# Piece size of loads, order of weight transfers and slot size in a fused linear-attention and mixture-of-experts kernel

## The chip, the cores and the metric

The kernel runs on one core of one Trainium2 chip. The metric is the device time of one execution in microseconds. Other engines than TensorE (PE) are named as the profile names them: DVE (VectorE), ACT (ScalarE), POOL (GpSimd), SP (SyncE).

## The reference

Linear attention with decay over blocks of 64 positions, then a top-1 mixture of experts on its output. Batch 4, 8 heads, 768 positions, head size 64; that makes 3072 tokens of 512 numbers, 8 experts with a hidden size of 1024.

```python
for b in range(nb):                       # blocks of 64 positions
    intra = (qb @ kb.T * Dmask) @ vb      # Dmask[i, j] = lam ** (i - j) for i >= j
    inter = (qb * lam_pow) @ kv_state
    out[:, :, block] = intra + inter
    kv_state = lam ** 64 * kv_state + (kb * rev_pow).T @ vb
x = out.transpose(0, 2, 1, 3).reshape(3072, 512)
logits = x @ w_gate + modality_bias[modality_id]
e_idx = argmax(logits); gate_w = softmax(logits)[e_idx]
for e in range(8):                        # each token goes to one expert
    out[mask] = gate_w[mask] * (relu(x[mask] @ w1[e]) @ w2[e])
```

## The kernel before, in words

**Attention stage.** The kernel works in 24 blocks of 128 positions (6 per batch element). A loop over steps `g` from 0 to 25 is a pipeline written out by hand: step `g` prepares block `g + 1` (`prepare`: two DVE products, `qd` on L200 and `kd` on L205), computes the scores of block `g` (`scores`, PE on L220, masks on DVE L223), the outputs of block `g - 1` (`from_state` L258, `outputs` L269, copies on ACT L271), adds to the state (`carry`, L235), and turns block `g - 2` into tokens (`tokens`): PE transposes them together with the router's product (L281), ACT copies the result to a tile `xn` (L282, three buffers), ACT's queue stores that tile to a table `xs` in HBM (L283, 256 KB), and DVE sums the logits (L285).

**Loads.** K, Q, V and a second layout of K lie together in the input `qkv`. One load (L180, on SP's queue) brings two blocks: a tile of 128 partitions with 16 KB each, contiguous in HBM. There are twelve such tiles in three buffers; the first comes in four parts (L68, L90), the next two follow in step 0, and from step 2 on every second step issues the load whose buffer the outputs of the step have just freed (the last, number 11, in step 18). In the same queue stand the two decay tables `dk` (L84, read from a small table that ACT's queue has written), and the filling of the slot table with an end mark (`inv<-pad`, L162, four transfers of 384 and 392 KB).

**Routing.** After the last block of a batch element `route` picks each token's expert on DVE, and a step later `route_places` works out each token's slot in its expert's list. `write_slots` then scatters 128 slots per call (POOL, L355) into the table `inv`, whose rows of `SW` = 16 words hold token number and gate weight. For two tiles of 256 tokens that can be formed from the first two batch elements, `early_list` (in step `early` = 14) makes a small list on DVE (`listA`): expert, place in `inv`, and whether the expert differs from the one before. SP reads such a list into registers (`value_load`, L517, L520, L495).

**Early tiles.** In step 18 SP fetches the two tiles' slots (`fetch_idx`, L500) and the first tile's `w1` (L525, four pieces of 512 KB into `raw1`), in step 20 its `w2` (L531, into `raw2`). POOL gathers the tokens (`fetch_rows`, L508). ACT and DVE split weights and tokens into a high and a low part (`split`, L482 and L483), and PE makes three products of each pair (`three`, L548, L551, L552).

**Expert stage.** `run(0)` and `run_early(1)` work the early tiles, two thin tiles of up to 64 tokens stand inside `run_early`, and `run(4)` and later ones work the wide tiles of 256 tokens. `run(0)` also places the last batch element's tokens and makes the list of all other tiles (`late_list`, DVE). `fetch_w1` and `fetch_w2` move nothing where the tile has the same expert as the one before; they are issued all the same. A thin tile uses plain products (`thin_first`, L578, `thin_second`, L600), and its weights come into `w1h` and `w1l` (`fetch_both`, L641, L644). `turn_rows` (L541) transposes the tokens of the next tile.

**What sets the order.** Each engine works its own instructions in the order that the build puts down. `behind(later, first)` orders two instructions: with `wait` the later one waits for the first one's end, without it the two are only put in this order.

Of the kernel before, what the change touches and what calls it, by code (L numbers as in the profile page):

```python
# [6 lines left out]
F32 = mybir.dt.float32  # L7
# [8 lines left out]
P = 128  # L16
B, H, S, D = 4, 8, 768, 64
NP = H // 2
NC = S // P
HB = 2  # L20
LOADS = 3
# [10 lines left out]
MAX_WIDE = 17  # L32
LIST = THIN + MAX_WIDE + 2
PAD = 4096
SW = 16
EMPTY = E * CAP // TT


def linear_attention_moe(tc, qkv, lam, modality, wg, mbias, w1, w2, out):
    nc = tc.nc  # L40
    with ExitStack() as ctx:
# [10 lines left out]
        def behind(later, first, wait=True):  # L52

            info = (mybir.DependencyInfo(mybir.DependencyClass.Sync, mybir.DependencyReason.DATA) if wait else
                    mybir.DependencyInfo(mybir.DependencyClass.NoSync, mybir.DependencyReason.SCHED_ONLY))
            tc.add_manual_dep(later.ins, first.ins.name, info, reason="order")
# [4 lines left out]

        def load_tile():

            return work.tile([P, HB, 4, H * D], F32, name="load", bufs=LOADS)

        first = load_tile()
        for part in (slice(0, 2), slice(2, 4)):
            nc.sync.dma_start(out=first[:, 0, part], in_=qkv[0, 0][:, 0, part])  # L68
        busy = const.tile([P, DM], BF16, name="busy")
        nc.vector.memset(busy, 0.0)  # L70
        tab = const.tile([H, 2 * P], F32, name="tab")
# [9 lines left out]

        dk = const.tile([P, 2, NP, P], F32, name="dk")
        for hl in range(2):
            tables = nc.sync.dma_start(  # L84
                out=dk[:, hl],
                in_=bass.AP(tensor=tab_d.tensor, offset=tab_d.offset + hl * 2 * P,
                            ap=[[1, P], [4 * P, NP], [1, P]]),
            )
        for part in (slice(0, 2), slice(2, 4)):
            ld = nc.sync.dma_start(out=first[:, 1, part], in_=qkv[0, 0][:, 1, part])  # L90
            behind(ld, tables, wait=False)
            tables = ld

# [81 lines left out]
        nc.vector.memset(ohsum, 0.0)  # L175

        def load_half(g):
            b, h = divmod(g, NC // HB)
            t = load_tile()
            behind(nc.sync.dma_start(out=t, in_=qkv[b, h]), tables, wait=False)  # L180
            return t

        halves = {0: first}

        def loaded(g):

            t = halves[g // HB][:, g % HB]
            kt, qt = (t[:, i].rearrange("p (a t) -> p a t", a=NP) for i in range(2))
            return kt, qt, t[:, 2], t[:, 3]

# [82 lines left out]

        def tokens(g, xt, lg):
            c = g % NC
            xn = work.tile([P, NP, P + E], F32, name="xn", bufs=3)
            for hf in range(2):
                xp = ps.tile([P, 2, 256], F32, name="x", bufs=2)
                for j in range(2):
                    p = hf * 2 + j  # L280
                    nc.tensor.matmul(xp[:, j, : P + E], xt[:, p, :], iw[:, p, :], start=True, stop=True)  # L281
                copies.append(nc.scalar.copy(out=xn[:, 2 * hf : 2 * hf + 2, :], in_=xp[:, :, : P + E]))  # L282
            nc.scalar.dma_start(out=xs[g * P : (g + 1) * P, :].rearrange("t (p d) -> t p d", p=NP),  # L283
                                in_=xn[:, :, :P])
            logits.append(nc.vector.tensor_reduce(out=lg[:, c, :], in_=xn[:, :, P:].rearrange("p q e -> p e q"),  # L285
                                                  axis=AX, op=ALU.add))
# [204 lines left out]
        def item(lst, row, i):  # L491
            return lst[0:1, row, i : i + 1] if isinstance(i, int) else lst[0:1, row, i]

        def fetch_idx(lst, i, idx, cols=TT):
            vr = nc.sync.value_load(item(lst, 1, i), min_val=0, max_val=E * CAP)  # L495
            if cols < TT:
                for p in range(0, P, cols):
                    nc.sync.dma_start(out=idx[p : p + cols, 0, :], in_=inv[bass.ds(vr, cols), 0:2])
                return
            nc.sync.dma_start(out=idx, in_=inv[bass.ds(vr, TT), 0:2].rearrange("(t p) c -> p t c", t=2))  # L500

        def groups(cols):

# [28 lines left out]
                if after is not None:  # L532
                    behind(ld, after)

        def turn_rows(cols, before=None):
            for i in range(2):
                tp = ps.tile([P, 2, TT], F32, name="x", bufs=2)
                for j in range(2):
                    kc = 2 * i + j
                    for t, m in groups(cols):  # L540
                        mm = nc.tensor.transpose(out=tp[:, j, t * P : t * P + m],  # L541
                                                 in_=xg[t][:m, kc * P : (kc + 1) * P], identity=ident[:m, :m])
                        if before is not None:
                            behind(mm, before, wait=False)
                split(tp[:, :, :cols], xh[i][:, :, :cols], xl[i][:, :, :cols])
# [150 lines left out]
        for g in range(0, ng + 2):  # L696
            if 1 <= g < ng - 1:
                st0[g + 1] = prepare(g + 1)
            if g == 2:
                routing_constants()  # L700
            if g < ng:
                st1[g], masked = scores(g)
            if g == 0:
                spread_powers()
                keep_busy(14)
                behind(nc.sync.dma_start(out=iw[:, :, P:], in_=wg), tables, wait=False)
                for i in range(1, LOADS):
                    halves[i] = load_half(i)
                for i in range(2):
                    st0[i] = prepare(i, masked)  # L710
            if 1 <= g <= ng:
                st2[g - 1], passed = outputs(g - 1, st1.pop(g - 1), from_state(g - 1, st0[g - 1][0]))
            if g < ng:
                passed = carry(g, st0[g][1]) or passed

            if g >= HB and g % HB == 0 and LOADS - 1 + g // HB < ng // HB:
                halves[LOADS - 1 + g // HB] = load_half(LOADS - 1 + g // HB)
            if g >= 2:
                b, c = divmod(g - 2, NC)
                if c == 0:  # L720
                    lgs[b] = work.tile([P, NC, E], F32, name="lg", bufs=2)
                tokens(g - 2, st2.pop(g - 2), lgs[b])
                if routed is not None:
                    slots = route_places(*routed)
                    routed = None
                if c == NC - 1:
                    routed = (b, *route(b, lgs.pop(b)))

            few = 2 if early <= g < early + 3 else 1
            write_slots(slots[:few], passed)  # L730
            slots = slots[few:]

            if g == early:
                exA, nA = early_list()
                er, _ = fetch_regs(listA, 0, True)
            elif g == early + 4:
                for i in range(EARLY):
                    fetch_idx(listA, i, idxA[i])
                fetch_w1(er, {})
            elif g == early + 6:  # L740
                fetch_w2(er, {})
            elif g == ng - 2:
                fetch_rows(idxA[0], TT, SOON * S, after=fades[-1])
            elif g == ng:
                split(raw1[0], w1h[0], w1l[0], late=True)
                turn_rows(TT)
            elif g == ng + 1:
                for i in range(1, 4):
                    split(raw1[i], w1h[i], w1l[i], late=True)
                fetch_w1(*fetch_regs(listA, 1, False))  # L750
                fetch_rows(idxA[1], TT, SOON * S)
# [11 lines left out]
        def regs(n):  # L763
            return fetch_regs(*tiles[n][1:], False)
# [21 lines left out]
        def run(n):  # L786
            idx = idxs.get(n) or get_idx(n)
            begun, turned = wide(tail, before)
            if n == 0:
                write_slots(route_places(*routed, begun))  # L790
                late_list(exA, nA)
            if n + 1 < fixed_ones:
                ahead = range(EARLY, wides + 1) if n == 0 else range(n + 2, min(n + 3, fixed_ones))
                for m in ahead:
                    idxs[m] = get_idx(m)
                fetch_w2(*regs(n + 1))
                turn_rows(TT, turned)
                for m in ahead:
                    gathered = rows_of(m)
                for i in range(4):  # L800
                    split(raw1[i], w1h[i], w1l[i])
                if n + 2 < fixed_ones:
                    fetch_w1(*regs(n + 2), gathered)
            second(idx)

        def run_early(n):
# [10 lines left out]
            fetch_w1(*regs(wides))  # L817
            other, mm = thin_first(xf[1], both[0])
            hnt = [thin_turn(hn, mm)]
            turn_rows(TT)  # L820
            gathered = rows_of(wides + 1)
            mm = thin_second(idxs[EARLY], hnt[0], raw2)
            hnt.append(thin_turn(other, mm))
            fetch_w2(*regs(wides))
            before = thin_second(idxs[EARLY + 1], hnt[1], both[1])
            w1h, w1l = parts(F32R)
# [75 lines left out]
```

## Time and profile before

| | us |
|---|---|
| median of 3 runs | 448.57 |
| lowest, highest | 447.22, 452.23 |
| profiled execution | 450.08 |
| its span | 448.3 |
| PE busy | 416.4 (93%) |
| DVE, ACT, POOL busy | 247.6, 188.1, 105.6 |

The mean granted clock of PE in the profiled execution is 0.973. The profile's page cuts the span into 40 slices of 11.2 us; a digit is the busy share of a slice in tenths, and PEclk the clock that PE was granted. In rows of the trace the first number is the start and the second the duration in us, then engine, line and operation, `out<-in`, and in brackets how long the engine sat idle before it and what ended that. An engine name with a q is that engine's instruction queue, for example while it issues a transfer.

The attention stage goes from the start to about 134 us, the early and thin tiles to about 205 us, the wide tiles to the end.

### The profile page before, as it was taken

How to read it: one execution, taken by the hardware profiler on the slowest of the kernel's cores; microseconds unless marked ns; L12 is line 12 of the kernel's file. 1: busy time of each engine (PE TensorE's matmuls, PEld its weight loads, DVE VectorE, ACT ScalarE, POOL GpSimd, SP SyncE). 2: the span in 40 equal slices, each digit the busy share in tenths (PEclk: the TensorE clock that was granted, in tenths of full speed). 3: DMA queues.
4: the chain of work that ended last, by engine and by line, in shares of the span. 5: the costliest groups of instructions: out<-in, count | busy, mean ns of one | idle time of the engine just before them, and what ended most of it. 6: DMA issues, size and time to landing. Idle time of an engine off the chain costs nothing.

```text
span 448.3 us, 9446 instructions
## 1 busy us (share of the span) xinstructions
PE 416.4 (93%) x3635; PEld 364.9 (81%) x3636; DVE 247.6 (55%) x481; ACT 188.1 (42%) x298; POOL 105.6 (24%) x110
## 2 busy tenths in 40 slices
PE   8899699899789998989999999999999999999980
PEld 4688588788669896759898999999998989898960
DVE  4686566756547946027837282919090919182510
ACT  1223133233158514134746363637272819182510
POOL 3110134431450343103221111313122221201010
PEclk9999889999898999999999999999999999999995
DMA  4999949778932012741112667530202020100000
GB/s 144 425 362 418 321 134 322 265 258 307 370 109 72 2 52 55 251 176 53 48 48 59 223 215 257 173 109 24 73 9 86 2 94 7 58 25 25 25 29 16
DMA packets 30356, 63.90 MB, mean 143 GB/s; under 512 B 6997, under 2 KB 20701, under 8 KB 28896
## 3 DMA queue, kind: packets, MB, share of 16 engines
q1 hardware_dynamic: 12816, 44.14, 27.7%
q0 software_dynamic: 4800, 12.79, 8.5%
q10 hardware_dynamic: 12688, 6.30, 4.7%
q8 instruction: 30, 0.49, 0.5%
q14 instruction: 22, 0.18, 0.1%
HBM read 91.04 MB, written 14.64 MB: 236 GB/s over the span
## 4 chain that ended last, share of the span: by engine, by line
issue 44%; PE 17%; DMA 16%; DVE 8%; POOL 7%; SPq 3%; ACT 1%; another core or an unknown queue 1%; POOLq 0%; ACTq 0%; DVEq 0%
DMA idx<-inv 4%; PE x L281 4%; POOL out_dram L622 4%; PE s L220 4%; PE o L269 4%; DMA xs<-xn 4%; POOL xg L508 3%; DMA xg<-xs,idx 3%; DMA load<-in_qkv_dram 2%; PE o L258 2%; DVE w1l L483 2%; DMA inv<-pay,sloti 2%; PE kv L235 2%; SPq L525 1%; DMA dk<-tab_d 1%
## 5 line engine op out<-in xcount | busy, mean ns | idle before, releaser
L548 PE MATMUL s<-xh,w1h 128*128 128x256 f32 x384 | 108.6, 283 | 0.8 <-issue 0.8
L551 PE MATMUL s<-xl,w1h 128*128 128x256 f32 x384 | 108.4, 282 | 0.0
L552 PE MATMUL s<-xh,w1l 128*128 128x256 f32 x384 | 108.2, 282 | 0.0
L483 DVE TENSOR_TENSOR w1l<-raw,w1h 128x1024 fp32r<-128x1024 f32 x48 | 58.0, 1220 | 75.1 <-ACT w1h L482 73.1
L551 PE MATMUL o<-w2l,hh 128*128 128x512 f32 x192 | 74.8, 390 | 2.0 <-DVE w2l L483 2.0
L548 PE MATMUL o<-w2h,hh 128*128 128x512 f32 x192 | 75.8, 395 | 0.0
L552 PE MATMUL o<-w2h,hl 128*128 128x512 f32 x192 | 74.9, 390 | 0.0
L548 PEld LDWEIGHTS s<-xh,w1h 128*128 128x128 f32 x384 | 72.6, 189 | 1.8 <-issue 1.4
L551 PEld LDWEIGHTS s<-xl,w1h 128*128 128x128 f32 x384 | 72.8, 190 | 0.4
L552 PEld LDWEIGHTS s<-xh,w1l 128*128 128x128 f32 x384 | 72.7, 189 | 0.1
L483 DVE TENSOR_TENSOR w2l<-raw,w2h 128x1024 fp32r<-128x1024 f32 x48 | 58.4, 1219 | 2.7 <-ACT w2h L482 2.2
L482 ACT CAST w1h<-raw 128x1024 fp32r<-128x1024 f32 x48 | 49.7, 1052 | 22.2 <-PE s L551 22.2
L482 ACT CAST w2h<-raw 128x1024 fp32r<-128x1024 f32 x48 | 49.8, 1041 | 0.1
L508 POOL DMA_INDIRECT xg<-xs,idx x20 | 27.7, 1383 | 83.7 <-PE x L541 80.0
L567 DVE SCALAR_TENSOR_TENSOR hl<-s,hh 128x512 fp32r<-128x512 f32 x48 | 32.9, 686 | 24.6 <-ACT hh L566 24.6
L621 ACT ACTIVATE y<-o,idx 128x512 f32<-128x512 f32 x20 | 13.8, 689 | 76.1 <-PE o L552 42.8
L622 POOL DMA_INDIRECT out_dram<-y,idx x20 | 21.4, 1068 | 101.0 <-ACT y L621 101.0
L551 PEld LDWEIGHTS o<-w2l,hh 128*128 128x128 f32 x192 | 36.1, 188 | 9.7 <-DVE w2l L483 2.5
L552 PEld LDWEIGHTS o<-w2h,hl 128*128 128x128 f32 x192 | 36.0, 188 | 7.5
L548 PEld LDWEIGHTS o<-w2h,hh 128*128 128x128 f32 x192 | 36.0, 188 | 7.1
L271 ACT COPY xt<-o 128x256 f32<-128x256 f32 x48 | 17.8, 372 | 54.8 <-PE o L269 47.9
L566 ACT ACTIVATE hh<-s 128x512 fp32r<-128x512 f32 x48 | 28.5, 594 | 23.2 <-PE s L552 13.7
(192 smaller groups left out, 505.4 us busy)
## 6 DMA issues: line engine op xcount, KB each, us to landing
raw<-in_w_dram SPq DMA_DIRECT2D x104, 512.0 KB
load<-in_qkv_dram SPq DMA_DIRECT2D x11, 2048.0 KB
xs<-xn ACTq DMA_DIRECT2D x24, 256.0 KB
load<-in_qkv_dram SPq DMA_DIRECT2D x4, 512.0 KB
w1h<-in_w_dram SPq DMA_DIRECT2D x4, 512.0 KB
w1l<-in_w_dram SPq DMA_DIRECT2D x4, 512.0 KB
inv<-pad SPq DMA_DIRECT2D x2, 392.0 KB
inv<-pad SPq DMA_DIRECT2D x2, 384.0 KB
```

The source lines that it names most:

```text
L220: nc.tensor.matmul(sps[hl][:, p, :], kt[r, p, :], qt[r, p, :], start=True, stop=True)
L269: mm = nc.tensor.matmul(op[half][place(p, hl), i, :], vt[:, (2 * p + hl) * D : (2 * p + hl + 1) * D], pts[hl][:, p, :], start=(c == 0 and ...
L281: nc.tensor.matmul(xp[:, j, : P + E], xt[:, p, :], iw[:, p, :], start=True, stop=True)
L482: cp = nc.scalar.copy(out=hi, in_=src)
L483: df = nc.vector.tensor_tensor(out=lo, in0=src, in1=hi.bitcast(F32), op=ALU.subtract)
L508: last = nc.gpsimd.indirect_dma_start(out=(to or xg)[t][:m], out_offset=None, in_=xs[:rows, :], in_offset=bass.IndirectOffsetOnAxis(ap=idx ...
L548: mm = nc.tensor.matmul(out, ah, bh, start=first, stop=False)
L551: nc.tensor.matmul(out, ah, bl, start=False, stop=False)
L552: return nc.tensor.matmul(out, al, bh, start=False, stop=last)
L566: act = nc.scalar.activation(out=hh[i], in_=hp, func=AF.Relu)
L567: nc.vector.scalar_tensor_tensor(out=hl[i], in0=hp, scalar=0.0, in1=hh[i].bitcast(F32), op0=ALU.max, op1=ALU.subtract)
L622: sc = nc.gpsimd.indirect_dma_start(out=out, out_offset=bass.IndirectOffsetOnAxis(ap=idx[:, t, 0:1], axis=0), in_=y, in_offset=None, bound ...
```

## The change

- The input `qkv` is laid out with the four arrays apart, so that a load takes 4 KB contiguous pieces, four per partition, in place of one of 16 KB; the tile's axes follow. The first tile's four parts take 2 KB pieces. The bytes are the same.
- The first of the two `dk` tables is issued on ACT's queue, the second stays on SP's.
- `xn` has four buffers in place of three.
- Slots in `inv` have 8 words (32 bytes) in place of 16, which halves the fill with end marks.
- `early_list` and the reading of its first entry move from step 14 to step 15.
- The fetches of the early slots are ordered behind the last load, and the first early tile's `w1` and `w2` wait for the last load to land.
- In `run(0)` the second early tile's `w2` is issued ahead of the slot fetches of the next tiles in place of behind them.
- In `run_early` the transposes of the next tile are cut in two: the second half goes between the two second products of the thin tiles, and the gather of the tile after it behind that.

```diff
-SW = 16
+SW = 8
@@ load tiles
-            return work.tile([P, HB, 4, H * D], F32, name="load", bufs=LOADS)
+            return work.tile([P, 4, HB, H * D], F32, name="load", bufs=LOADS)
+
+        def source(g):
+            return qkv[divmod(g, NC // HB)].rearrange("x p c f -> p x c f")
...
-            nc.sync.dma_start(out=first[:, 0, part], in_=qkv[0, 0][:, 0, part])
+            nc.sync.dma_start(out=first[:, part, 0], in_=source(0)[:, part, 0])
...
-            tables = nc.sync.dma_start(
+            tables = (nc.scalar, nc.sync)[hl].dma_start(
                 out=dk[:, hl],
...
-            behind(nc.sync.dma_start(out=t, in_=qkv[b, h]), tables, wait=False)
+            ld = nc.sync.dma_start(out=t, in_=source(g))
+            behind(ld, tables, wait=False)
+            loads.append(ld)
...
-            xn = work.tile([P, NP, P + E], F32, name="xn", bufs=3)
+            xn = work.tile([P, NP, P + E], F32, name="xn", bufs=4)
@@ fetch_idx(lst, i, idx, cols=TT, after=None)
-            nc.sync.dma_start(out=idx, in_=inv[bass.ds(vr, TT), 0:2].rearrange("(t p) c -> p t c", t=2))
+            ld = nc.sync.dma_start(out=idx, in_=inv[bass.ds(vr, TT), 0:2].rearrange("(t p) c -> p t c", t=2))
+            if after is not None:
+                behind(ld, after, wait=False)
@@ the loop over steps
-            if g == early:
+            if g == early + 1:
                 exA, nA = early_list()
                 er, _ = fetch_regs(listA, 0, True)
             elif g == early + 4:
                 for i in range(EARLY):
-                    fetch_idx(listA, i, idxA[i])
-                fetch_w1(er, {})
+                    fetch_idx(listA, i, idxA[i], after=loads[-1])
+                fetch_w1(er, {}, loads[-1])
             elif g == early + 6:
-                fetch_w2(er, {})
+                fetch_w2(er, {}, loads[-1])
@@ run(n)
+                if n == 0:
+                    fetch_w2(*regs(n + 1))
                 for m in ahead:
                     idxs[m] = get_idx(m)
-                fetch_w2(*regs(n + 1))
+                if n > 0:
+                    fetch_w2(*regs(n + 1))
@@ run_early(n)
-            turn_rows(TT)
-            gathered = rows_of(wides + 1)
+            turn_rows(TT, part=(0,))
             mm = thin_second(idxs[EARLY], hnt[0], raw2)
             hnt.append(thin_turn(other, mm))
+            turn_rows(TT, mm, part=(1,))
+            gathered = rows_of(wides + 1)
@@ host: layout of qkv
-        "qkv": c(_np.stack([cols(kr), cols(inputs["q"]), rows(vr), rows(kr)], axis=4)),
+        "qkv": c(_np.stack([cols(kr), cols(inputs["q"]), rows(vr), rows(kr)], axis=2)),
```

More of the change, by code (lines that the diff above doesn't have):

```diff
@@ L89, in linear_attention_moe @@
         for part in (slice(0, 2), slice(2, 4)):
-            ld = nc.sync.dma_start(out=first[:, 1, part], in_=qkv[0, 0][:, 1, part])
+            ld = nc.sync.dma_start(out=first[:, part, 1], in_=source(0)[:, part, 1])
             behind(ld, tables, wait=False)
@@ L177, in load_half @@
         def load_half(g):
-            b, h = divmod(g, NC // HB)
             t = load_tile()
-            behind(nc.sync.dma_start(out=t, in_=qkv[b, h]), tables, wait=False)
+            ld = nc.sync.dma_start(out=t, in_=source(g))
+            behind(ld, tables, wait=False)
+            loads.append(ld)
             return t
-        halves = {0: first}
+        halves, loads = {0: first}, []
         def loaded(g):
-            t = halves[g // HB][:, g % HB]
+            t = halves[g // HB][:, :, g % HB]
             kt, qt = (t[:, i].rearrange("p (a t) -> p a t", a=NP) for i in range(2))
@@ L492, in item, with fetch_idx @@
             return lst[0:1, row, i : i + 1] if isinstance(i, int) else lst[0:1, row, i]
-        def fetch_idx(lst, i, idx, cols=TT):
+        def fetch_idx(lst, i, idx, cols=TT, after=None):
             vr = nc.sync.value_load(item(lst, 1, i), min_val=0, max_val=E * CAP)
@@ L533, in fetch_w2, with turn_rows @@
                     behind(ld, after)
-        def turn_rows(cols, before=None):
-            for i in range(2):
+        def turn_rows(cols, before=None, part=range(2)):
+            for i in part:
                 tp = ps.tile([P, 2, TT], F32, name="x", bufs=2)
```

## The prediction

> **What bounds the kernel now.** I read the page's slices first, then PE's waits, then windows of whole steps, and last the DMA queues in the stretches where PE waits. The slices of 11.2 us:
>
> ```profile
> PE   8899699899789998989999999999999999999980
> ...
> PEclk9999889999898999999999999999999999999995
> ```
>
> From slice 19 on (205 us) PE is full and its clock whole; nothing there can be gained by moving transfers. The holes lie before: slices 4 and 10, the dips of the clock beside them, 11 to 12 and 15 to 17. The list of PE's waits (total, times, longest, in us) names them:
>
> ```profile
> PE kv L235 <- DVE state L244: 3.2, 1, 3.2
> PE x L326 <- ACT xn L282: 2.2, 1, 2.2
> PE x L281 <- ACT xn L282: 2.1, 1, 2.1
> PE o L551 <- DVE w2l L483: 2.0, 1, 2.0
> ...
> PE x L365 <- DVE ohsum L350: 1.2, 1, 1.2
> ...
> PE o L600 <- DVE hnt L589: 0.8, 1, 0.8
> ...
> PE x L541 <- DVE hnt L589: 0.3, 1, 0.3
> ```
>
> To price them with all they drag along I cut the attention stage at the starts of the token transposes (L281) of blocks 5, 7, 11, 14, 18 and 22 (columns: PE busy, weight loads, DVE, ACT, POOL, each with its count of instructions, then granted clock, DMA share, GB/s):
>
> ```profile
> 42.90:59.00 16.10, 11.77 (x155) 10.33 (x151) 10.03 (x31) 2.92 (x10) 3.19 (x3) 0.79 0.82 276
> 59.00:75.10 16.10, 16.10 (x260) 14.24 (x256) 10.39 (x21) 5.99 (x16) 6.16 (x6) 1.00 0.74 241
> 75.10:91.40 16.30, 14.42 (x229) 12.27 (x224) 12.81 (x56) 4.42 (x14) 7.63 (x8) 1.00 0.80 269
> 91.40:108.30 16.90, 16.43 (x261) 14.25 (x257) 11.98 (x29) 6.57 (x18) 3.53 (x4) 1.00 0.84 270
> 108.30:129.10 20.80, 17.59 (x249) 15.01 (x247) 8.79 (x26) 5.44 (x16) 7.34 (x8) 0.92 0.82 304
> ```
>
> The second row has no hole: 260 matmuls in 16.10 us, 62 ns each. At that pace the others need 155 x 0.062 = 9.6, 229 x 0.062 = 14.2, 16.2 and 15.4 us. They last 6.5, 2.1, 0.7 and 5.4 us longer: **14.7 us** of the attention stage is waiting, clock dips included.
>
> The 6.5 us. ACT wants to copy block 5 into a buffer of `xn` from 43.0 us on (48.94 less 5.98), and block 2's store to `xs`, which reads that buffer, has not landed:
>
> ```profile
> 32.17 0.52 ACTq L283 DMA_DIRECT2D xs<-xn  x1
> ...
> 48.94 0.67 ACT L282 COPY xn<-x 128x272 f32<-128x272 f32 x2 [5.98 <-DMA xs<-xn]
> ```
>
> Why a 256 KB store takes over 16 us is told by the DMA answer for 36 to 40 us (packets, MB, share of 16 engines) and, as the case with 4 KB pieces, for 113 to 121 us, where expert weights load:
>
> ```profile
> q1 hardware_dynamic: 100, 1.59, 93.8%
> q10 hardware_dynamic: 95, 0.05, 4.0%
> ```
>
> ```profile
> DMA packets 1606, 3.25 MB, mean 407 GB/s; under 512 B 112, under 2 KB 915, under 8 KB 1605
> ...
> q1 hardware_dynamic: 781, 2.84, 86.8%
> q10 hardware_dynamic: 817, 0.41, 17.0%
> ```
>
> q1 is SP's queue, q10 ACT's. Both times the queues take turns packet by packet, 100 to 95 and 781 to 817. A turn of q1 costs 93.8% x 64 / 100 = 0.60 us with 16 KB, 86.8% x 128 / 781 = 0.14 us with 4 KB (some tiny packets among them). A store has 512 packets of 512 B, 32 per engine, at 17.0% x 128 / 817 = 0.027 us each: beside loads it needs up to 32 x 0.6 = 19 us.
>
> [...]
>
> The 5.4 us. The last load waits for L269 of step 18, which frees its buffer at 99.2 us, but is issued 4 us later, behind an index fetch that sits in SP's queue until the slot scatters have landed, and behind two weight pieces:
>
> ```profile
> 98.09 1.09 PE L269 MATMUL o<-pt,load 128*64 128x128 f32 x16
> ...
> 100.88 0.98 SPq L500 DMA_DIRECT2D idxA<-inv  x2
> 102.05 1.08 SPq L525 DMA_DIRECT2D raw<-in_w_dram  x2
> 103.26 0.34 SPq L180 DMA_DIRECT2D load<-in_qkv_dram  x1
> ...
> 130.63 1.05 ACT L482 CAST w1h<-raw 128x1024 fp32r<-128x1024 f32 x1
> ```
>
> ```profile
> 103.26 10.95 DMA load<-in_qkv_dram
> ```
>
> By the chain it takes 10.95 us with weights beside it, lands at 114.2, and PE stands 3.2 us (L235).
>
> **The change part by part.**
>
> *4 KB pieces and a fourth `xn`.* The same bytes; a load of 2.1 MB takes 5.2 us at 407 GB/s; by 100 packets of 16 KB in 4 us it now takes 5.1. A store beside loads needs 32 x (0.14 + 0.03) = 5.5 us of turns instead of 19. With four buffers it is block 6, a step of 4.0 us after block 5, that waits for block 2's store: at 47.0 us, by when the store of 32.17 has had 15 us. Of the 6.5 us I take **6.2**; late next would be the load after it, of which no wait shows before 81 us. If the store were as slow as now, 48.9 - 47.0 = 1.9 us of the wait would stay.
>
> *Loads ahead, weights behind the last one.* The last load goes at 99.2 and, without the two weight pieces (1.05 MB, 2.6 us at 407 GB/s) ahead of it, in 8.4 to 10.95 us: it lands between 107.6 and 110.2, 4 to 6.6 us sooner. The 4.2 MB of early weights wait for that landing and take some 10 us at 407 GB/s: about 120, with 10 us to the cast at 130.63 that wants them first. Behind that new wait on SP's queue stand only more weights. The stores on ACT share the engines with the weights, as they did. Of the 5.4 us I take **4.6**, bounds 2 and 5.4.
>
> *The early list one step later.* It removes the wait of L365 (1.2 us), which sits in the row 75.1 to 91.4 with two late loads, this and a later one:
>
> ```profile
> 81.16 0.69 DVE L200 TENSOR_TENSOR qd<-load,pq 128x512 f32<-128x512 f32 x1 [1.22 <-DMA load<-in_qkv_dram]
> 101.07 0.69 DVE L200 TENSOR_TENSOR qd<-load,pq 128x512 f32<-128x512 f32 x1 [2.19 <-DMA load<-in_qkv_dram]
> L517 SPq TENSOR_LOAD <-listA x3: 4/264/476, 87.4 to 90.7; - x3
> ...
> L520 SPq TENSOR_LOAD <-listA x2: 262/320/379, 90.0 to 91.3; - x2
> ```
>
> The twenty small DVE operations of the list only move by a step, and SP's reads of the list (L517, L520) come closer to the next load. I take **1.0** of the 2.1 (bounds -2 and 2.1), and **0.4** of the 0.7 in the next row.
>
> *The start.* One decay table goes to ACT's queue, the first tile comes in 2 KB pieces, the pads halve.
>
> ```profile
> 6.95 0.94 SPq L84 DMA_DIRECT2D dk<-tab_d  x2
> ...
> 15.84 12.41 SPq L162 DMA_DIRECT2D inv<-pad  x4
> ...
> 21.04 0.38 PE L220 MATMUL s<-load 64*128 64x128 f32 x2 [0.72 <-DMA load<-in_qkv_dram]
> ```
>
> SP is half of 0.94 us earlier with all that follows, the second load's arrival (21.04) among it; 2 KB pieces, which no row shows, lie between the 4 KB and 512 B rows, so up to 0.3 us back. ACT waits for the table before its next issue, but its next work (the first copies) comes after 9 us. The pads, 1.55 MB less 0.78, free 1.9 us of DMA and SP's queue ahead of a load that PE hardly misses. **0.4**, bounds -0.3 and 1.3. Slots of 32 bytes: a scatter writes 128 rows either way, and no load waits for its landing any more, so 0.
>
> *Second early tile.* Its weight fetch goes ahead of the index fetches:
>
> ```profile
> 169.17 3.14 SPq L531 DMA_DIRECT2D raw<-in_w_dram  x4
> 176.30 1.30 SPq L525 DMA_DIRECT2D raw<-in_w_dram  x4
> ...
> 180.74 2.52 SPq L641 DMA_DIRECT2D w1h<-in_w_dram  x4
> ```
>
> ```profile
> SPq L525 <- DMA xg<-xs,idx: 38.0, 10, 11.0
> ```
>
> ```profile
> 191.72 1.49 PEld L578 LDWEIGHTS s<-w1h,xf 128*64 128x64 f32 x14 [0.63 <-DMA w1h<-in_w_dram]
> ```
>
> L551's 2.0 us go. But then PE reaches the thin tile 2 us sooner, and there it already waits for `w1h`, whose issue stands behind L525 at 176.30 on SP, and L525 waits for the gathers, which nothing moves. So the stall shifts to L578: **0.3**, bounds 0 and 2.0. The transposes split around the thin tile cover L541's 0.3 and L600's 0.8 us; the same matmuls and casts run: **0.8** of 1.1.
>
> Sum: 6.2 + 4.6 + 1.0 + 0.4 + 0.4 + 0.3 + 0.8 = **13.7 us**. The profiled execution took 450.1 us (span 448.3), so 436.4 by its own time; from the median 448.6 it is 434.9. I forecast **435**.
>
> **The rivals.**
>
> *SP's queue still makes a load late.* The reads of the list (87.4 to 91.6 us) stand ahead of the load of step 16 in SP's queue, and they come a step, 4.0 us, later now. DVE waited 2.19 us for that load as it was (101.07), so each us of delay costs one: up to 4, with the 1.0 gained in that row gone too, 435 + 5 = 440. For it: the order on SP is fixed by the program, not by what is free. Against: loads should land up to 1 us sooner with weights and starved stores out of their way. Chance 0.20.
>
> *The pieces do not do what they are for.* The store of 32.17 sends nothing before 36: the answer for 32 to 36 us has
>
> ```profile
> q1 hardware_dynamic: 116, 1.69, 100.8%
> ```
>
> and no q10. If an engine always finishes what it has taken of a load before it turns to the store, 4 KB changes little, and the fourth buffer alone helps: 1.9 us of the wait stay, 437. Against it: from 36 us on the rows show a store getting its turns in the middle of a load. Chance 0.10. [...]
>
> *Slower: the loads become the bound.* With 32 pieces per engine a load gives 32 turns to each of two stores, 2 x 32 x 0.027 = 1.7 us, and 0.3 us by its own rate: 2.0 us. From step 6 on, nine loads have no more slack than the waits above show; if each comes 2 us late, 18 us are lost against 13.7 won: 453. It decides from 13.7 / 9 = 1.5 us per load. Against: the stores' bytes were paid for before as well, behind the load, and 113 to 121 us ran at 407 GB/s with both. Chance 0.05.
>
> On the clock: between 42.9 and 59 it falls (0.79) after waits of 2.1 and 2.2 us, so I count it back with them. [...]
>
> **How the numbers follow.** Forecast 0.65, SP's queue 0.20, pieces 0.10, loads 0.05. Lowest: all of 14.7, 1.3 at the start and 3.1 behind, 19.1, gives 429. Highest without the slower case: the row bounds 2 for 4.6 and -2 for 1.0 give 435 + 5.6, and 2 us of a load late beside it, 443. 429 to 443 leaves out the slower case and some tails, under 0.2. One per cent, 4.5 us, is about what can be told from no change: above 444 lie 0.05 slower and some of the rivals' tails, 0.07 within. Faster 0.88.
>
> **What the profile would show.** PE waits at L281 and L326 on `xn` gone, and the window from block 5 to 7 near 9.8 us; the last load issued before the index fetch, and no 3 us wait at L235; clock whole from 10 us to the handover near 118; L551's wait gone and a longer one at L578; loads' packets 4 KB with q10 at least even. Wrong would make it: a DVE or PE wait on a load of over 2 us in blocks 13 to 20, a store that blocks ACT behind weights, or a handover to the experts that waits for the weights moved back.

## The result and the profile after

| | before | after |
|---|---|---|
| median, us | 447.89 | 430.77 |
| lowest, highest | 445.23, 452.23 | 429.88, 431.68 |
| profiled execution | 450.08 | 429.88 |
| its span | 448.3 | 428.2 |
| PE busy | 416.4 (93%) | 410.2 (96%) |
| mean granted clock | 0.973 | 0.988 |

The ratio is 0.9637 (95% interval 0.9585 to 0.9689). It is that of the means of the fast executions, 447.0 and 430.8 us, so the slow one of 452.23 us is not in it, and by it the change is worth 16.2 us. By the medians it is 17.1 us, by the spans of the two profiled executions 20.1 us. The forecast was 435, with a range of 429 to 443.

The page of the changed kernel, PE and its clock in 40 slices (10.7 us each):

```profile
PE   8999999999989999999999999999999999999980
...
PEclk9999999999999999999999999999999999999995
```

All dips of the clock are gone ahead of the last slice, and the one thin slice left between the start and the end is the handover to the experts. The list of PE's waits, changed kernel (total, times, longest, us):

```profile
PE o L694 <- DVE busy L73: 1.3, 1, 1.3
PE x L285 <- DVE xl L487: 1.0, 1, 1.0
PE s L554 <- ACT xh L486: 0.8, 1, 0.8
PE o L606 <- DVE hnt L595: 0.7, 2, 0.3
PE s L224 <- DMA load<-in_qkv_dram: 0.4, 1, 0.4
...
```

The three waits left out are of 0.2 to 0.3 us each. No wait for the state, for `xn`, for the one-hot sums or for `w2l` is left. The windows of the same block steps as in the prediction (5 to 7, 7 to 11, 11 to 14, 14 to 18, 18 to 22), changed kernel:

```profile
42.20:52.10 9.90, 9.71 (x154) 8.39 (x152) 9.69 (x32) 2.83 (x9) 1.62 (x2) 1.00 0.99 359
52.10:68.20 16.10, 16.10 (x260) 14.24 (x256) 11.61 (x25) 6.01 (x17) 6.96 (x7) 1.00 0.91 292
68.20:82.30 14.10, 14.10 (x228) 12.34 (x224) 11.26 (x39) 4.79 (x14) 7.18 (x8) 1.00 0.93 321
82.30:98.50 16.20, 16.20 (x261) 14.26 (x257) 13.21 (x47) 6.36 (x18) 3.81 (x4) 1.00 0.95 312
98.50:114.30 15.80, 15.80 (x249) 13.64 (x247) 8.66 (x26) 5.61 (x16) 7.32 (x8) 1.00 0.94 328
```

The second row, which had no hole, has not moved. The others are 6.2, 2.2, 0.7 and 5.0 us shorter, 14.1 of the 14.7 us of waiting that the prediction found there.

### The profile page after: what moved, and what is told of

The parts are those of the page before. It is cut to its first block, busy times and chain, and to the rows that moved or that the text cites. A ratio compares the mean times of both kernels' runs of the same rounds, so it can differ in the third digit from the quotient of the medians.

```text
span 428.2 us, 9453 instructions
## 1 busy us (share of the span) xinstructions
PE 410.2 (96%) x3635; PEld 361.3 (84%) x3636; DVE 246.6 (58%) x481; ACT 188.1 (44%) x298; POOL 104.4 (24%) x110
## 4 chain that ended last, share of the span: by engine, by line
issue 43%; PE 32%; DMA 10%; POOL 7%; DVE 3%; SPq 2%; POOLq 0%; ACT 0%; DVEq 0%
PE s L224 6%; PE x L285 6%; PE o L273 5%; DMA idx<-inv 4%; POOL out_dram L628 4%; DMA xg<-xs,idx 3%; POOL xg L514 3%; DMA load<-in_qkv_dram 3%; PE o L262 3%; PE kv L239 2%; PE o L554 2%; PE o L557 2%; PE o L558 2%; PE s L558 2%; PE s L557 2%
## 5 line engine op out<-in xcount | busy, mean ns | idle before, releaser
L514 POOL DMA_INDIRECT xg<-xs,idx x20 | 29.3, 1463 | 83.7 <-PE x L547 80.1
L628 POOL DMA_INDIRECT out_dram<-y,idx x20 | 20.3, 1014 | 100.8 <-ACT y L627 100.8
L573 DVE SCALAR_TENSOR_TENSOR hl<-s,hh 128x512 fp32r<-128x512 f32 x48 | 32.9, 685 | 15.6 <-ACT hh L572 15.6
```

Source lines behind the costliest of these rows:

```text
L514: last = nc.gpsimd.indirect_dma_start(out=(to or xg)[t][:m], out_offset=None, in_=xs[:rows, :], in_offset=bass.IndirectOffsetOnAxis(ap=idx ...
L573: nc.vector.scalar_tensor_tensor(out=hl[i], in0=hp, scalar=0.0, in1=hh[i].bitcast(F32), op0=ALU.max, op1=ALU.subtract)
L628: sc = nc.gpsimd.indirect_dma_start(out=out, out_offset=bass.IndirectOffsetOnAxis(ap=idx[:, t, 0:1], axis=0), in_=y, in_offset=None, bound ...
```

## The experiments

Two theories stood at first for the 6.2 us of blocks 5 to 7. **Theory 1**: the two queues take turns packet by packet, so 16 KB pieces starve the stores; small pieces and the fourth buffer are each nearly enough. **Theory 2**: only the fourth buffer matters. The first four runs made a third necessary, given behind them. In the table, the last column is the difference of ratio from the control, times 449 us. With intervals of 0.3 to 0.5% on each ratio, a difference under some 3 us is not told by the times alone; there the trace has to speak, and one trace against the others, since a stretch can move by itself.

| run | against the changed kernel | median, us | ratio to before (95%) | us |
|---|---|---|---|---|
| e1_control | nothing | 431.35 | 0.9641 (0.9590-0.9691) | 0 |
| e2_big_pieces | 16 KB pieces | 431.86 | 0.9651 (0.9605-0.9697) | +0.4 |
| e3_three_xn | three `xn` | 432.22 | 0.9652 (0.9601-0.9704) | +0.5 |
| e4_big_three_xn | both | 433.39 | 0.9690 (0.9641-0.9739) | +2.2 |
| e6_big_xn3_sw16 | both, slots of 64 bytes | 442.29 | 0.9852 (0.9807-0.9896) | +9.5 |
| e7_after_late_scores | step 6 in before's order | 433.54 | 0.9673 (0.9633-0.9713) | +1.4 |
| e12_only_fourth_xn | 16 KB, slots of 64 bytes | 433.89 | 0.9661 (0.9619-0.9702) | +0.9 |
| e8_weights_ahead | early weights not behind the last load | 439.12 | 0.9782 (0.9741-0.9822) | +6.3 |
| e9_list_step_14 | list back in step 14 | 434.24 | 0.9658 (0.9610-0.9706) | +0.8 |
| e10_second_w2_behind | `w2` behind the slot fetches | 433.86 | 0.9677 (0.9635-0.9720) | +1.6 |
| e11_turn_whole | transposes in one piece | 433.72 | 0.9643 (0.9612-0.9674) | +0.1 |
| e5_before_order | (the kernel before, step 6 in the new order) | 446.30 | 0.9944 (0.9917-0.9971) | |

The runs came in three groups of four (e1 to e4, e5 to e8, e9 to e12), each on a chip of its own, with the kernel before at 447.75, 449.25 and 449.11 beside them.

**Pieces and buffers.**

```diff
-        "qkv": ... axis=2      # and the tile's axes: loads of 4 KB pieces
+        "qkv": ... axis=4      # e2, e4: one piece of 16 KB
-            xn = work.tile([P, NP, P + E], F32, name="xn", bufs=4)
+            xn = work.tile([P, NP, P + E], F32, name="xn", bufs=3)   # e3, e4
```

> The changed kernel itself, beside its variants on the same chip: 430 to 431.5 us, a span near 428, the windows of the x transposes of blocks 5 to 7 near 9.9 us.

> The changed kernel with the loads of steps 1 to 11 back in 16 KB pieces; the fourth xn buffer stays. Theory 1 (the two queues' packets take turns one for one, so stores of 512 B pieces get a 512th part of the time beside 16 KB pieces; pieces and fourth buffer are each nearly enough): the store of block 2 again waits for load 3 and the stores are late by some 15 us, but the fourth buffer takes all except about 2 us of it: +1 to +3 us, with a wait of L285 or L281 on xn near blocks 5 to 7. Theory 2 (only the fourth buffer matters, the packets do not): within 0.5 us of the control and the stores no later than there.

> The changed kernel with three xn buffers; the 4 KB pieces stay. Theory 1: the stores keep going 4 to 5 us apart, the store of block 2 is over before the copy of block 5 wants its buffer: 0 to +1.5 us. Theory 2 (only the fourth buffer matters): the window of blocks 5 to 7 is back near 16 us and the time goes up by 5 to 6.5 us.

> Both undone: 16 KB pieces and three xn buffers, all else as changed. Both theories: the window of blocks 5 to 7 goes back to about 16 us and the dip of the granted clock near 52 to 58 us is back: +6 to +7 us, 436.5 to 438. By how far this is more than the sum of the two single undoings tells that the two edits cover the same wait.

The control came out as the changed kernel had. Neither edit taken back alone changes the time beyond the noise. Both together come out 2.2 us slower, which is not told from nothing either, and is not the 6 to 7 expected. (The 512th part in the expectation for e2 is a slip: in the first rows of e4 below the store has 3.6% of the time against 97.3%, a 27th.) The one long wait that e3 has and the changed kernel has not lies at the handover:

```profile
PE x L547 <- ACT xn L286: 1.3, 1, 1.3
```

The window of blocks 5 to 7 in e4_big_three_xn:

```profile
43.20:52.50 9.30, 9.30 (x155) 8.14 (x151) 9.09 (x30) 2.90 (x10) 1.62 (x2) 1.00 0.98 368
```

The stall is not back, with the pieces and the buffers of before. Both theories miss it: something else in the change removes it. The order of PE's rows differs. First the kernel before, then e4_big_three_xn, PE in step 6 (start, duration, engine, line; scores are L220 and L224, outputs L269 and L273):

```profile
36.09 1.09 PE L269 MATMUL o<-pt,load 128*64 128x128 f32 x16
37.51 1.16 PE L220 MATMUL s<-load 64*128 64x128 f32 x16 [0.33 <-DMA load<-in_qkv_dram]
```

```profile
36.35 1.16 PE L224 MATMUL s<-load 64*128 64x128 f32 x16 [1.34 <-DMA load<-in_qkv_dram]
...
38.04 1.09 PE L273 MATMUL o<-pt,load 128*64 128x128 f32 x16
...
39.19 8.33 SPq L182 DMA_DIRECT2D load<-in_qkv_dram  x2
```

Before, the outputs of block 5 stood ahead of the scores of block 6 and did not wait for the load that these need. Their end frees the buffer of load 5, which therefore went at 37.23 us. Now the scores stand first, wait 1.34 us, and load 5 goes at 39.19. In the changed kernel they stand first too (35.27 us, outputs 36.96), but its load 3 is there in time, and load 5 goes at 38.10. What the 2 us do in e4 is told by the DMA answers of e4_big_three_xn for 36 to 40 and for 40 to 41.4 us (packets, MB, share), and by that of e6_big_xn3_sw16, below, for 40 to 41.4 us:

```profile
q1 hardware_dynamic: 88, 1.44, 97.3%
q10 hardware_dynamic: 86, 0.04, 3.6%
```

```profile
q10 hardware_dynamic: 711, 0.36, 84.6%
q1 hardware_dynamic: 18, 0.05, 9.6%
```

```profile
q1 hardware_dynamic: 39, 0.56, 92.9%
q10 hardware_dynamic: 137, 0.07, 16.4%
```

Beside load 4 the store gets its one turn per 16 KB packet in e4 as in before. But between loads 4 and 5 there is a gap now, in which 711 store packets go; 512 make a whole store. In e6 load 5 follows at once (issued at 36.50 us): only 137 go in the same stretch, and ahead of that stretch, from 37.5 to 39.5 us, it is one small packet per large one (49 to 49). So I put up **Theory 3**: a late load 5, small pieces and a fourth buffer are three covers for one stall.

**The order.** For e5 two order edges (without a wait) were put into the kernel before; for e7 the scores of step 6 are put down behind the outputs in the changed kernel; in e6 and e12 the slots' size brings back before's order in step 6 by itself.

```diff
# e5, in from_state and in tokens of the kernel before
+                            if g == 5:
+                                behind(mm, last_score[6], wait=False)
+                    if g == 4:
+                        behind(mm, carried, wait=False)     # transposes of block 4 behind carry of 6
# e6, e12, beside 16 KB pieces (and, in e6, three xn)
-SW = 8
+SW = 16
# e7, loop over steps
-            if g < ng:
+            if g < ng and g != 6:
                 st1[g], masked = scores(g)
...
+            if g == 6:
+                st1[g], masked = scores(g, passed)          # ordered behind outputs(5)
```

> The kernel before with one thing changed: PE's order in step 6, where the scores of block 6 now stand ahead of the two halves of the outputs of block 5, as they do in the changed kernel (before they stood behind them, and so the buffer of load 5 came free 2 us sooner). Pieces of 16 KB, three xn buffers and slots of 64 bytes stay. Theory 3 (the order decides: load 5 then starts after load 4 has ended, the stores get the gap between them, and the copy of block 5 finds its buffer free): the waits on xn near 47 and 51 us and the clock dip go, the window of blocks 5 to 7 is 9.5 to 11 us, and the time falls by 5 to 6.5 us against before. Theory 1 (pieces or fourth buffer are needed): within 1 us of before.

> The changed kernel with three things undone: 16 KB pieces, three xn buffers and slots of 64 bytes, with which PE's order in step 6 is again that of before. Theory 3: the slots are what changed the order; the waits on xn are back, the window of blocks 5 to 7 is near 16 us, 4 to 6 us over the kernel with only pieces and buffers undone (433.4), so 437.5 to 439.5. If the slots do not matter: 433 to 434.

> The changed kernel, whole, except that PE's order in step 6 is put back to that of before (scores of block 6 behind the outputs of block 5). Theory 3 with theory 1 as its second half (pieces and fourth buffer cover the same wait as the order does): 0 to +1.5 us over the changed kernel, the stores no longer than 8 us, no wait on xn. If pieces and buffer cover nothing: +5 to +6.5 us.

> The changed kernel with 16 KB pieces and slots of 64 bytes (so PE's order in step 6 is that of before), but with the fourth xn buffer. The prediction's second rival worked out here: the store of block 2 takes 14 us as before and lands near 46, block 6 waits for it from 47 us or hardly at all, so 0 to 2 us of the wait stay: +0.5 to +3 us over the changed kernel, against +9.5 us without the fourth buffer. If the buffer does not help because the next copy meets the same stores: +5 us and more.

e6 differs from e4 only in the slots, and takes 7.3 us more (9.5 less 2.2), where 4 to 6 were expected. Its rows of PE and of ACT, and its window of blocks 5 to 7:

```profile
35.36 1.09 PE L273 MATMUL o<-pt,load 128*64 128x128 f32 x16
36.60 1.16 PE L224 MATMUL s<-load 64*128 64x128 f32 x16
...
47.80 0.67 ACT L286 COPY xn<-x 128x272 f32<-128x272 f32 x2 [5.76 <-DMA xs<-xn]
```

```profile
42.00:57.30 15.30, 11.51 (x156) 9.97 (x152) 10.01 (x31) 2.81 (x10) 3.18 (x3) 0.78 0.85 294
```

Order, ACT's wait and the dip of the clock are those of before. So the 32-byte slots, for which the prediction had 0, change PE's order in step 6. Counted matmul by matmul, PE's order in e4 and e6 is the same everywhere else, but for one matmul of the outputs and one of the carry that change places at 88.5 us, as they do in e8 with the small slots; e2 and e12 differ in the same way. Why the build orders it so was not tried; the fill of the slot table stands ahead of load 3 in SP's queue, and its size is the only thing that differs in that queue. Not all of the 7.3 us is this stall: from block 3 to block 7 e6 takes 4.9 us more than e4 (23.6 against 18.7), and 1.7 us more lie at the handover, at a wait for `xn` (L547) of 2.0 us in place of 0.4.

The buffer works without the new order, and so do the pieces and the buffer together. With before's order, e7 (4 KB pieces, four buffers) has these DMA rows for 36 to 40 us and this copy of block 5, e12 (16 KB, four buffers) this wait and window:

```profile
q1 hardware_dynamic: 325, 1.32, 87.1%
q10 hardware_dynamic: 322, 0.16, 13.6%
```

```profile
42.99 0.85 ACT L288 COPY xn<-x 128x272 f32<-128x272 f32 x2 [0.73 <-PE x L287]
```

```profile
49.14 0.18 PE L330 MATMUL x<-oh,lowb 128*128 128x48 bf16 x1 [0.63 <-ACT xn L286]
```

```profile
42.60:52.60 10.00, 9.37 (x156) 8.26 (x152) 9.86 (x31) 3.10 (x10) 2.53 (x3) 1.00 1.05 366
```

With small pieces the store sends 322 packets in these 4 us, where it sent 95 in before and 175 in e6, and ACT waits for nothing but PE. With the buffer alone 0.63 us of waiting stay. From block 3 to block 7 it is 24.6 us before and 23.6 in e6, but 18.7 in e4 (late load 5 alone), 18.7 in e12 (buffer alone), 18.0 in e7 (pieces and buffer) and 18.0 in the changed kernel. So Theory 3 holds for the late load and for the buffer. That the pieces alone would cover the stall is not shown: pieces without the fourth buffer in before's order were not run.

In the kernel before, the order alone brings 2.5 us (1.3 to 3.7 by the interval), not 5 to 6.5. The windows of e5 from block 3 to block 5 and from 5 to 7, and what PE waited for:

```profile
34.40:46.80 12.40, 9.68 (x131) 8.53 (x129) 5.83 (x12) 3.44 (x10) 0.62 (x1) 0.86 0.97 350
46.80:56.30 9.50, 9.33 (x154) 8.22 (x152) 9.26 (x29) 2.96 (x9) 1.82 (x3) 1.00 0.97 338
```

```profile
38.31 1.44 PE L221 MATMUL s<-load 64*128 64x128 f32 x16 [2.72 <-DMA load<-in_qkv_dram]
```

Blocks 5 to 7 run free, as Theory 3 has it, but the scores that now stand first wait 2.72 us for load 3, where e4 waited 1.34, and the clock dips there. From block 3 to 7 it is 21.9 us against 24.6 before (34.4 to 59.0). The expectation left out that the new order has a price of its own, the wait for load 3. In the changed kernel that wait is not there; which of its edits brings load 3 earlier was not tried.

**Weights behind the last load.**

```diff
-                    fetch_idx(listA, i, idxA[i], after=loads[-1])
-                fetch_w1(er, {}, loads[-1])
+                    fetch_idx(listA, i, idxA[i])
+                fetch_w1(er, {})
...
-                fetch_w2(er, {}, loads[-1])
+                fetch_w2(er, {})
```

> The changed kernel with the early slots' fetches no longer ordered behind the last load, and the early weights no longer waiting for it. By the prediction's term (4.6 of 5.4 us): the last load is issued 3 to 5 us later, stands behind weights, a wait of PE at the carry or the scores of some 3 us is back and the clock dips near 115 us: +3.5 to +5 us, 435 to 436.5. Rival (what made the last load late was a slow chain ahead of it, which is gone with the stores): 0 to +1 us.

SP's issues from 92 us on, a wait of PE, and the window of blocks 18 to 22, all of e8:

```profile
92.25 1.93 SPq L504 DMA_DIRECT2D idxA<-inv  x2
94.36 0.35 SPq L531 DMA_DIRECT2D raw<-in_w_dram  x1
94.89 0.38 SPq L182 DMA_DIRECT2D load<-in_qkv_dram  x1
```

```profile
PE kv L239 <- DVE state L248: 3.0, 1, 3.0
```

```profile
100.60:122.50 21.90, 18.87 (x251) 16.02 (x247) 8.59 (x26) 5.55 (x16) 7.32 (x8) 0.84 0.82 305
```

The last load stands behind the index fetch and a weight piece again, PE waits 3.0 us, and the window is 6.1 us longer than the changed kernel's 15.8; in all other runs of the changed kernel it takes 15.9 to 16.1. The times say 6.3. That is above the 3.5 to 5 expected, but by less than the noise. In the trace the window is 1.1 us longer than before the change (20.8), with PE busy 1.3 us longer (18.87 against 17.59) at a lower clock (0.84 against 0.92). In the changed kernel the last two loads go first:

```profile
81.99 8.51 SPq L182 DMA_DIRECT2D load<-in_qkv_dram  x2
90.79 1.75 SPq L504 DMA_DIRECT2D idxA<-inv  x2
99.12 3.38 SPq L531 DMA_DIRECT2D raw<-in_w_dram  x4
```

**The early list.**

```diff
-            if g == early + 1:
+            if g == early:
                 exA, nA = early_list()
```

> The changed kernel with the early list, and the reading of its first entry, back in step 14. By the prediction's terms (1.0 and 0.4): the wait of PE at the one-hot sums (L369) of 1.2 us is back, the stretch from block 11 to block 18 is 1 to 1.5 us longer, +1 to +1.5 us over the changed kernel. By the windows of the changed kernel (2.2 and 0.7 us shorter than before): +2 to +3 us. If the list moved nothing and the stores were what shortened these windows: within 0.5 us.

The windows of blocks 11 to 14 and 14 to 18 in e9:

```profile
68.70:84.40 15.70, 14.45 (x228) 12.18 (x224) 12.03 (x55) 4.40 (x14) 7.63 (x8) 1.00 0.86 284
84.40:100.90 16.50, 16.43 (x260) 14.26 (x257) 12.06 (x29) 6.55 (x18) 3.52 (x4) 1.00 0.91 301
```

The wait at the one-hot sums is back, smaller than before:

```profile
76.00 0.18 PE L369 MATMUL x<-ohsum,onesb 128*128 128x8 bf16 x1 [0.70 <-DVE ohsum L354]
```

The windows are 1.6 and 0.3 us longer than in the changed kernel, 1.9 together: between the two expectations. But the first of them moves by itself: with the list in step 15 it takes 14.1 us in e1, e2 and e4, 14.6 in e7, e10 and e11, and 15.6 in e6, e8 and e12. Only the wait of 0.70 and the 0.3 us of the second (16.1 in all these runs) are shown to be the list's. The times (+0.8) do not tell it from nothing.

**The second early tile's w2.**

```diff
-                if n == 0:
-                    fetch_w2(*regs(n + 1))
                 for m in ahead:
                     idxs[m] = get_idx(m)
-                if n > 0:
-                    fetch_w2(*regs(n + 1))
+                fetch_w2(*regs(n + 1))
```

> The changed kernel with the second early tile's w2 issued behind the slot fetches again. By the prediction (0.3, the stall only shifts to the thin tile's first weights): L557 waits 1.6 to 2.2 us again, the thin tile starts later by that but the wait for w1h of 0.6 us does not come, and the time rises by 0 to 0.5 us. Rival (those first weights come early by themselves now, since the list and with it the queue's reads are done sooner, so nothing takes the place of the wait): +1.8 to +2.5 us.

```profile
159.88 0.50 PE L557 MATMUL o<-w2l,hh 128*128 128x512 f32 x1 [1.00 <-DVE w2l L487]
174.44 1.73 PE L584 MATMUL s<-w1h,xf 128*64 128x256 f32 x14 [0.98 <-DMA w1h<-in_w_dram]
```

Both waits of e10's PE come together, 1.00 and 0.98 us, where the changed kernel has neither, so here the one does not take the other's place. The edit's own part is clean: from PE's transposes of the thin tiles' tokens (`x<-ident,xq`, L640) to the thin tile's first product it is 13.2 us in e10, and 11.9 in the changed kernel and in each of the other ten runs that have `w2` ahead. That makes 1.3 us, between the two expectations. The issue of the thin tile's weights is not so clean. The first row is of e10, the second of the changed kernel:

```profile
165.56 2.84 SPq L647 DMA_DIRECT2D w1h<-in_w_dram  x4
```

```profile
163.74 2.10 SPq L647 DMA_DIRECT2D w1h<-in_w_dram  x4
```

Counted from the same transposes (156.18 and 155.36 us) that is 9.4 and 8.4 us, and the runs with `w2` ahead go from 7.1 (e1) to 9.8 (e9). Nor is the wait for `w1h` e10's alone: it is 1.1 us in e6, 0.4 in e7, 0.6 in e8, 2.3 in e9, 0.8 in e11 and 1.0 in e12, all with `w2` ahead, and it is missing in e1 to e4. What decides it, no run shows.

**The transposes in one piece.**

```diff
-            turn_rows(TT, part=(0,))
+            turn_rows(TT)
+            gathered = rows_of(wides + 1)
             mm = thin_second(idxs[EARLY], hnt[0], raw2)
             hnt.append(thin_turn(other, mm))
-            turn_rows(TT, mm, part=(1,))
-            gathered = rows_of(wides + 1)
```

> The changed kernel with the transposes of the next tile in one piece ahead of the thin tiles' second products. By the prediction (0.8 of 1.1): a wait of 0.7 to 0.8 us at L606 and of 0.3 at the transposes are back in place of two of 0.35 us, +0.3 to +0.8 us, below what the times can tell; the trace has to show it.

PE of e11 from the turn of the first thin tile (L593) to the first wide product:

```profile
178.91 0.66 PE L593 MATMUL x<-ident,hn 128*128 128x128 f32 x4
...
185.98 3.67 PE L606 MATMUL o<-w1l,hnt 128*64 128x256 f32 x32 [0.78 <-DVE hnt L595]
189.58 0.39 PE L554 MATMUL s<-xh,w1h 128*128 128x256 f32 x1
```

The stretch takes 10.67 us, as in before. In the changed kernel it is 10.09, as in every other run with the split:

```profile
174.46 0.66 PE L593 MATMUL x<-ident,hn 128*128 128x128 f32 x4
...
184.55 0.39 PE L554 MATMUL s<-xh,w1h 128*128 128x256 f32 x1
```

The split is worth 0.6 us, within the 0.3 to 0.8 expected and, as expected, invisible in the times (+0.1).

## Why the prediction was right, and where not

The working read the waits and their sizes rightly, and the time lies in the range. The sum was 2.5 us short by the means of the result, 3.4 by the medians and 6.4 by the profiled executions, and one cause was missed.

| step | foreseen, us | between the two profiles | by undoing it |
|---|---|---|---|
| pieces and fourth `xn` (blocks 5 to 7) | 6.2 | 6.2 | 0.7 from block 3 to 7, 2.2 in the times, within the noise (e4) |
| weights behind the last load (18 to 22) | 4.6 | 5.0 | 6.1 to 6.3 (e8) |
| early list (11 to 14, 14 to 18) | 1.4 | 2.9 | 0.7 and 0.3 (e9) |
| start | 0.4 | 0.7 | not undone |
| slots of 32 bytes | 0 | in the first row | the order alone 1.4, within the noise (e7); 4.9 from block 3 to 7 and 7.3 in the times with e4's two edits undone (e6) |
| second early tile | 0.3 | 2.4 ahead of the thin tile, 0.7 in it | 1.3 (e10) |
| transposes split | 0.8 | 0.6 | 0.6 (e11) |

- **Pieces and fourth buffer.** The size is exact, and the two edits are enough for it: in before's order, e7 has the window of the changed kernel (9.9 us). The turns of the two queues are shown (88 to 86, 325 to 322). What the working did not see is that the two edits are not needed for it: with the new order they add 0.7 us from block 3 to block 7. In before's order the buffer alone would nearly do it: e7 and e12 are 8.1 and 8.6 us faster than e6. The rival that the pieces do nothing and 1.9 us stay is refuted for its first half by e7's packets; for the buffer alone 0.6 us stayed.
- **Slots of 32 bytes.** Here the reasoning failed, though the 0 did little harm. It counted rows written and bytes moved, and not that the build puts PE's instructions in another order. On top of the pieces and the buffer that order is worth at most e7's 1.4 us; without them it is most of the 7.3. The result alone could not show it, since the term of the pieces and the buffer stood for the same wait; that the missed cause was covered by it is luck.
- **Weights.** Foreseen 4.6 of 5.4; 5.0 came. The last load was issued at 90.1 us, as its buffer came free, and the weights that wait for its landing at 99.1, so it took 9.0 us, within the 8.4 to 10.95 of the working.
- **Early list.** The window of 14 to 18 lost its whole 0.7 us, that of 11 to 14 2.2. Of these 2.9 e9 shows 1.0 to be the list's, so that the 1.4 foreseen was near; the rest lies in a window that takes 14.1 to 15.6 us without any edit to the list. The rival of SP's queue (a load 4 us late) did not come about: loads 10 and 11 were issued at 82.0 and 90.1 us, each as its buffer came free, and the reads of the list (84.8 to 88.9 us) fell between them.
- **Second early tile.** The term was mis-sized: 0.3 foreseen, 1.3 by e10 and 2.4 between the two profiles ahead of the thin tile. The step gave the gain away again by "the stall shifts to L578". In the changed kernel it did not shift. From the thin tile's first product to its turn (L593) it is 7.9 us before, 7.2 in the changed kernel and 7.1 to 7.4 in e1 to e4, but 8.3 to 10.2 in e6 to e9, e11 and e12, which have `w2` ahead too. So the stall can come there as the step said, and in the profiled execution of the changed kernel it did not; the cause stays open.
- **Slower rival.** Loads did not become the bound: PE's waits for loads sum to 0.4 us.
- **The rest of the 20.1 us.** From the first product of the early tiles to the transposes at L640 it is 39.2 us before and 37.9 in the changed kernel. These 1.3 us were not in the sum; they are the clock behind the handover, 0.83 in before (128 to 138 us) and 1.00 after (112 to 138 us). Another 0.4 us lie behind the first wide product. The clock there is scatter: with the same work e1, e7, e9 and e10 take 37.9 us there, and e2, e3, e4, e8, e11 and e12 38.8 to 39.1; in windows of 5 us behind the handover the clock is 1.00 in the first four and falls to 0.66 to 0.83 in the others. e2_big_pieces and e7 have the same two waits there (0.8 and 1.0 us), and these rows, for 120 to 125 us, first e2's and then e7's:

```profile
120.00:125.00 5.00, 5.00 (x32) 4.99 (x32) 2.47 (x10) 3.41 (x5) 1.01 (x1) 0.70 0.51 158
```

```profile
120.00:125.00 5.00, 4.66 (x40) 4.45 (x39) 3.52 (x13) 4.40 (x7) 1.02 (x1) 1.00 0.54 157
```

  The profiled executions also lie 2.2 us above and 0.9 below their medians (450.08 and 447.89, 429.88 and 430.77), which is the 3 us between 20.1 and 17.1.

Equal counts alone (88 to 86, 325 to 322) would also come of long turns with as many records on either side. But in the profile of before, in each 0.3 us from 36 to 39.9 us, there are 4 to 11 records of q10 and 3 to 11 of q1. The small ones come spread out, with none of these stretches empty, so the rows speak for turns of one record or a few.

## What to carry to other kernels

A resize of a side table can reorder another engine's instructions, as the slots did between e4 and e6: compare the order of each engine before and after, not only the operations that the diff names. Here a small-packet store beside large-packet loads got one turn per large packet where the loads left no gap (88 to 86); a buffer more, smaller pieces together with that buffer, or a gap between the loads each kept most of the wait away (blocks 5 to 7 took 10.0 us in e12, 9.9 in e7 and 9.3 in e4, against 15.3 in e6). When several edits aim at one wait, undo them together as well as one by one, or each will look worthless. And before a stretch that got longer is put down to an edit, look at the same stretch in the runs that do not have it: the blocks 11 to 14 and the wait for `w1h` moved by 1.5 and 2.3 us from run to run by themselves.

## What was not expected of the hardware

The gap mattered more than the turns: with loads of 16 KB pieces beside it the store sent 86 packets in 4 us, in the 1.4 us between two loads 711 (e4). And the clock fell behind the handover in some executions and not in others behind waits of the same length: 0.70 in e2 and 1.00 in e7, after 0.8 and 1.0 us with matmuls between the two, with the difference unexplained.
